# Attention followed by a two-layer MLP on one core: the first rows of k and q come in two pieces, k's first in float32 by another queue

## The chip, the cores and the metric

The kernel runs on one core of one Trainium2 chip. The metric is device time in microseconds (us) of one execution; less is better. Engines are named as in the profile: PE (TensorE, matmuls; PEld its weight loads), DVE (VectorE), ACT (ScalarE), POOL (GpSimd), SP (SyncE). PE writes to PSUM, in banks of 128 x 512 float32; DVE and ACT read PSUM; DMAs move data between device memory and SBUF.

## The reference

Sliding-window attention with a linear bias per head, then an MLP with an ELU between its two products. B = 8 batches, H = 8 heads, S = 576 positions, D = 64; 4608 tokens, 512 model columns, 2048 hidden columns. Inputs and output are float32.

```python
def _attn_ref(q, k, v):
    window, scale = 128, 1.0 / np.sqrt(D)
    scores = scale * np.matmul(q, k.transpose(0, 1, 3, 2))
    rel = pos[:, None] - pos[None, :]
    slopes = 2.0 ** (-8.0 * (np.arange(H) + 1) / H)
    bias = slopes[:, None, None] * (-np.abs(rel))[None, :, :]
    mask = (rel >= 0) & (rel < window)
    scores = np.where(mask, scores + bias[None], -1e9)
    attn = softmax(scores)                     # written out with max, exp and sum
    return np.matmul(attn, v)

x = attn_out.transpose(0, 2, 1, 3).reshape(B * S, H * D)
h = x @ w_in
g = np.where(h > 0, h, np.exp(np.minimum(h, 0)) - 1)
out = g @ w_out
```

## The kernel before, in words

**Attention.** A query block of 128 positions sees its own key block and the one before. The kernel goes by key blocks, called units: unit u takes keys 128u to 128u+127 and the 256 queries from 128u on (unit 3 takes the last rows with it). For batches 0 and 1 q and k are loaded with their rows in the partitions (tiles `s0`), turned on PE by 64 x 64 or 128 x 128 transposes into PSUM (`turn_first`, L136) and copied to the tiles QT and KT, with the head dimension in the partitions (L140). For the other batches DVE turns them (`turn_qk`).

The bias of batch 0 is added on PE: a matmul of a scaled identity (`SI`) with a table `RB` of distances and mask (`early_bias`, L183; `bias`, L166). Scores are added on top (`early_scores`, L191; `first_scores`, L176), ACT takes the exponential with the factor 1/8 out of PSUM (`early_expo`, L197 and L200; `first_expo`), and PE multiplies with v (`values`, L253), where a column of ones in v gives the sums, by which DVE divides (L259, L260). `turn` transposes the result (L289) and copies it to the tile `xT` (L290), block by block of 128 tokens. Later batches don't add the bias: they multiply the exponentials by a table `TAB` (`first_weigh`, `weigh`), which ACT makes from `RB` with one exponential per head (L471).

**MLP.** A step of `hidden` (L305) multiplies a block of `xT` with a part of w_in into one PSUM bank; in the early steps ACT takes the exponential (L315), POOL clamps it (L316) and DVE makes the ELU (`elu`, L323). `output` (L329), for the first 256 tokens, and after them `product` (L393, a form of the second product with seven half-size products in place of eight) multiply with w_out; `put` and `store` write the results by SP's queue.

**Order.** Nothing is scheduled by a planner: the order is written out by hand and each engine runs its instructions in that order. First comes a prologue: loads, masks, 22 matmuls on a constant tile that give PE something to do (`warm`), then units 0 and the first half of unit 1 of batch 0 in 128-query halves, with their values. Then a loop over numbered slots: each slot runs its `hidden` step, the ELU of the step before, the tasks that `at(slot, ...)` has put there, and the outputs. Steps 0 to 7 use w_in's four column parts for token blocks 0 and 1 in turn: steps 0 and 1 the first part, 2 and 3 the second, and so on.

**Loads at the start.** All go through POOL's queue, which casts float32 to float16 on the way, in this order: k rows 0 to 255, (iota for the masks), q rows 0 to 255, v blocks 0 and 1, w_in part 0, q rows 256 to 383, k rows 256 to 575, q rows 384 to 575, w_in parts 1 and 2, v block 2, and after some memsets w_in part 3 and v blocks 3 and 4. `split(b, w, part)` gives the pieces: start partition, number of partitions, rows to a partition, first row, and place in the tile. SP's queue does nothing before 41 us.

In the prologue k's two halves of heads (`half`) are turned into PSUM banks hp[0] and op and copied by DVE; q's into hp[1], copied by ACT, and av, copied by DVE. PSUM banks are named sp[0] to sp[3] (AB is the first two), hp[0], hp[1], av and op.

Of the kernel before, what the change touches and what calls it, by code (L numbers as in the profile page):

```python
# [18 lines left out]
def kernel(  # L19
# [9 lines left out]
    nc = tc.nc  # L29
# [60 lines left out]
    def split(b, w, part):  # L90

        if b == 0 and w == 1:
            return ((0, 64, 4, 0, 0), (64, 64, 5, 256, 0))[part]
        if b == 0:
            return ((0, 64, 4, 0, 0), (64, 64, 2, 256, 0), (64, 64, 3, 384, 2))[part]
        return ((0, 128, 4, 0, 0), (0, 64, 1, 512, 4))[part]

    def load_first(b, w, part):

        p0, n, m, r0, j0 = split(b, w, part)  # L100
        nc.gpsimd.dma_start(
            s0[b][p0:p0 + n, w, :, j0:j0 + m, :].rearrange("p h j d -> p h (j d)"),
            (q, k)[w][b, :, r0:r0 + n * m, :].rearrange("h (p j) d -> p h (j d)", j=m))

    def load_qk(b, w, g):
        if b not in st:
# [5 lines left out]
    def load_v(b, n):  # L112
        p = 128 if n < 4 else 64
        nc.gpsimd.dma_start(VP[b % 2][0:p, n, :, 0:D],  # L114
                            v[b, :, 128 * n:128 * n + p, :].rearrange("h p d -> p h d"))

    def load_wi(i):
        c = slice(512 * i, 512 * i + 512)
        nc.gpsimd.dma_start(w_in_sb[:, :, c], moe_w_in[:, c].rearrange("(c p) f -> p c f", p=128))
# [4 lines left out]
            moe_w_out[512 * i:512 * i + 512, :].rearrange("(c p) d -> p c d", p=128))  # L124


    def turn_first(b, w, part, half, bank, copy):

        p0, n, m, r0, j0 = split(b, w, part)
        nh = 4 if n * m < 256 else 2  # L130
        t = bank.bitcast(F16)[:, 0:nh * m * n].rearrange("p (x j r) -> p x j r", x=nh, j=m)
        r = slice(p0, p0 + n)
        for x in range(nh):
            for j in range(m):
                for hh in range(2):
                    nc.tensor.transpose(t[64 * hh:64 * hh + 64, x, j, :], s0[b][r, w, 4 * hh + nh * half + x, j0 + j, :],  # L136
                                        ident[r, r])
        t = t.rearrange("p x j r -> p x r j")
        o = (Q0, K0)[w][b][:, nh * half:nh * half + nh, r0:r0 + m * n]
        copy(o.rearrange("p x (r j) -> p x r j", j=m), t)  # L140
# [6 lines left out]
    nc.scalar.preload_act_table_set("natural_log_exp_and_others")  # L147

    with tc.manual_schedule():

# [26 lines left out]
        def early_bias(banks, c0):  # L179

            for x in range(4):
                for hh in range(2):
                    nc.tensor.matmul(banks[hh][:, 128 * x:128 * x + 128], SI[:, 4 * hh + x, :], RB[:, c0:c0 + 128],  # L183
                                     start=x == 0, stop=False, skip_group_check=True)

        def early_scores(banks, u, c0):
            k0, q0 = 128 * u, 128 * u + c0
            for x in range(4):
                for hh in range(2):
                    r = slice(64 * hh, 64 * hh + 64)  # L190
                    nc.tensor.matmul(banks[hh][:, 128 * x:128 * x + 128], kt_[0][r, x * S + k0:x * S + k0 + 128],  # L191
                                     Q0[0][r, x, q0:q0 + 128], start=False, stop=True, skip_group_check=True)

        def early_expo(banks, u, c0):
            e = ex_[u][:, 0:2048].rearrange("p (h c) -> p h c", h=8)[:, :, c0:c0 + 128]
            if banks is AB:
                nc.scalar.activation(e, spa.rearrange("p g (h c) -> p (g h) c", h=4), AF.Exp, scale=0.125)  # L197
                return
            for hh in range(2):
                nc.scalar.activation(e[:, 4 * hh:4 * hh + 4, :], banks[hh].rearrange("p (h c) -> p h c", h=4),  # L200
                                     AF.Exp, scale=0.125)
# [41 lines left out]
        def values(b, i, part, bank=av):  # L243

            m = 128 if i < 4 else 64
            banks = (part, part + 2) if b < 2 else (2 * part, 2 * part + 1)
            parts = [(3, 128, 3), (3, 192, 4)] if i == 4 else [(i, 0, i)] + ([(i - 1, 128, i - 1)] if i else [])
            a = bank[:, 0:4 * (D + 1)].rearrange("p (x h d) -> p x h d", x=2, h=2)
            for x, g in enumerate(banks):
                for h2 in range(2):  # L250
                    for j, (u, c, n) in enumerate(parts):
                        c += 512 * g + 256 * h2
                        nc.tensor.matmul(a[:, x, h2, :], ex_[u][:, c:c + 128], VP[b % 2][:, n, 2 * g + h2, 0:D + 1],  # L253
                                         start=j == 0, stop=j == len(parts) - 1)
            if part == 0:
                xnt[b, i] = work.tile([128, 4, 2, D], F16, name="xn", tag="xn", bufs=4)
            o = xnt[b, i][0:m, part::2, :, :] if b < 2 else xnt[b, i][0:m, 2 * part:2 * part + 2, :, :]
            r = work.tile([128, 2, 2], F32, name="rden", tag="rden", bufs=2)
            V.reciprocal(out=r[0:m], in_=a[0:m, :, :, D])  # L259
            V.tensor_tensor(out=o, in0=a[0:m, :, :, 0:D], in1=r[0:m].unsqueeze(3).broadcast_to([m, 2, 2, D]),  # L260
                            op=ALU.mult)
# [138 lines left out]
        def combine(n, what):  # L400
            late = n >= 2 * NTB - 2
            if what == "C11":
                add(tile_out(n, 0)[:, 0:256], kept(n, 1), place(n, 2))
                if late:
                    put(n, 0, 0, 256)
            elif what == "C12":
                add(tile_out(n, 0)[:, 256:512], kept(n, 6), place(n, 3))
                put(n, 0, 256 if late else 0, DO)
            else:
                add(tile_out(n, 1)[:, 256:512], kept(n, 7), kept(n, 5))  # L410
                if n == 2 * NTB - 2:
                    put(n, 1, 0, 256)
                put(n, 1, 256 if late else 0, DO)

        def put(n, i, c0, c1, queue=nc.sync):
            r = 256 * n + 128 * i
            queue.dma_start(out[r:r + 128, c0:c1], tile_out(n, i)[:, c0:c1])
# [11 lines left out]
        def warm(n, bank=op):  # L429
            for _ in range(n):  # L430
                nc.tensor.matmul(bank[:, 0:256], wz[:, 0:128], wz, start=True, stop=True)
# [3 lines left out]
        rel = fore[3][:, 1536:2048].bitcast(I32)  # L435
        far = fore[1][:, 0:256]
        V.memset(wz, 1.0)
        load_first(0, 1, 0)
        nc.gpsimd.iota(rel, pattern=[[1, 256]], base=0, channel_multiplier=-1)
        load_first(0, 0, 0)  # L440
        load_v(0, 0)
        load_v(0, 1)
        load_wi(0)
        load_first(0, 0, 1)
        load_first(0, 1, 1)
        load_first(0, 0, 2)
        load_wi(1)
        load_wi(2)
        load_v(0, 2)
# [17 lines left out]
            V.tensor_scalar(out=SI[:, h, :], in0=ident, scalar1=8.0 * slope[h], scalar2=None, op0=ALU.mult)  # L467
        V.memset(VP[0][:, :, :, D:D + 1], 1.0)

        for h in range(H):  # L470
            nc.scalar.activation(TAB[:, 0, h // 2, h % 2, :], RB[:, 0:256], AF.Exp, scale=slope[h])  # L471
        warm(22)
        turn_first(0, 1, 0, 0, hp[0], V.tensor_copy)
        turn_first(0, 1, 0, 1, op, V.tensor_copy)
        early_bias(AB, 0)
        turn_first(0, 0, 0, 0, hp[1], nc.scalar.copy)
        turn_first(0, 0, 0, 1, av, V.tensor_copy)
        V.tensor_copy(RB[:, 256:448], RB[:, 0:192])
        V.tensor_copy(RB[:, 448:512], RB[:, 0:64])
        V.tensor_copy(TAB[:, 1, :, :, 0:192], TAB[:, 0, :, :, 0:192])  # L480
        V.tensor_copy(TAB[:, 1, :, :, 192:256], TAB[:, 0, :, :, 0:64])
        early_bias(sp[2:4], 128)
        early_scores(AB, 0, 0)
        early_expo(AB, 0, 0)
        early_scores(sp[2:4], 0, 128)
        early_expo(sp[2:4], 0, 128)
        early_bias((hp[1], av), 0)
        early_scores((hp[1], av), 1, 0)
        early_expo((hp[1], av), 1, 0)
        values(0, 0, 0, hp[0])  # L490
# [2 lines left out]
        turn(0, 0, V.tensor_copy, hp[0])  # L493
        values(0, 1, 0)
        values(0, 1, 1, op)


        early, tasks, late, HID, OUT = {}, {}, {}, {}, {}

        def at(s, f, *a):  # L500
            tasks.setdefault(s, []).append((f, a))
# [39 lines left out]


        at(0, turn, 0, 1, V.tensor_copy)
        at(0, turn_first, 0, 0, 1, 0, sp[3], nc.scalar.copy)
        before(1, done, 0)
        at(1, early_bias, AB, 128)
        at(1, early_scores, AB, 1, 128)
        at(1, early_expo, AB, 1, 128)
        at(1, turn_first, 0, 1, 1, 0, av, V.tensor_copy)
        at(1, turn_first, 0, 1, 1, 1, sp[2], nc.scalar.copy)  # L550
        at(1, turn_first, 0, 0, 2, 0, hp[0], V.tensor_copy)
        for half in range(2):
            at(1, bias, 2, half, 3 * half)
        for half in range(2):
# [10 lines left out]
        at(5, first_scores, 0, 3, 1, 0)  # L565
        at(5, first_expo, 0, 3, 1, 0, 0, 256)
        at(5, done, 4)
        at(9, values, 0, 3, 0)
        at(9, values, 0, 3, 1, sp[3])
        at(10, values, 0, 4, 0)  # L570
# [135 lines left out]
```

## Time and profile before

| | us |
|---|---|
| median of 3 runs (lowest, highest) | 310.12 (309.92, 310.66) |
| the profiled execution | 310.72 |
| its span, from first to last instruction | 308.9 |
| PE busy in it | 300.8 |
| DVE, ACT, POOL busy | 258.0, 241.5, 108.5 |
| PE's first transpose of k, first of q | 6.00, 8.29 |
| MLP steps 0, 1, 2 start on PE | 13.61, 15.78, 20.37 |

A timeline line of the profile gives start, time busy, engine, source line and operation, the tile written and the tiles read, shape, count of merged instructions, and in brackets the idle time ahead of it with what ended it. DMA lines give the KB that are written and the time from issue to landing. Loads from POOL's queue are counted by their float16 size.

### The profile page before, as it was taken

What the parts mean: (1) busy time and instruction counts of PE and PEld (TensorE: products, weight loads), DVE (VectorE), ACT (ScalarE), POOL (GpSimd) and SP (SyncE); (2) the same over time, 40 slices, a digit from 0 to 9 for tenths busy, and PEclk for the clock granted to TensorE, in tenths of its full rate; (3) what the DMA queues carried; (4) which work ended last, traced back from release to release, by engine and by line L of the source; (5) the groups of instructions that cost most, each with busy time, mean ns of one, the idle gap of its engine ahead of it and who ended that gap; (6) DMA issues with size and microseconds to landing.
All of it is one profiled execution on the core that took longest, in us unless ns stands there. A gap on an engine that the chain in (4) does not pass through costs nothing.

```text
span 308.9 us, 9842 instructions
## 1 busy us (share of the span) xinstructions
PE 300.8 (97%) x4079; PEld 256.5 (83%) x4079; DVE 258.0 (84%) x499; ACT 241.5 (78%) x445; POOL 108.5 (35%) x163
## 2 busy tenths in 40 slices
PE   7899999999999999999999999999999999999996
PEld 5688775798788888988888888888899888888885
DVE  5646887988989999997989998989998788886783
ACT  4576678778889698879797889788988797968881
POOL 8938868274261415140707060806000101010000
PEclk9999999999999999999999999999999999999999
DMA  9999999999197929495979997999620302030103
GB/s 95 188 198 201 201 176 189 92 118 122 23 153 73 152 55 149 55 142 70 109 93 118 130 98 82 125 135 107 68 92 15 96 17 87 19 97 1 70 17 121
DMA packets 96941, 32.04 MB, mean 104 GB/s; under 512 B 83968, under 2 KB 92800, under 8 KB 96896
## 3 DMA queue, kind: packets, MB, share of 16 engines
q0 software_dynamic: 75920, 18.36, 64.8%
q1 hardware_dynamic: 20832, 12.98, 17.4%
q8 instruction: 32, 0.52, 0.7%
q14 instruction: 13, 0.11, 0.1%
q10 hardware_dynamic: 144, 0.07, 0.1%
HBM read 36.70 MB, written 9.44 MB: 149 GB/s over the span
## 4 chain that ended last, share of the span: by engine, by line
PE 76%; DVE 7%; ACT 6%; DMA 5%; issue 3%; POOL 2%; POOLq 0%; DVEq 0%; ACTq 0%
PE hp L305 34%; PE op L393 13%; PE av L393 12%; PE spa L225 4%; PE spa L271 3%; DVE g L323 2%; DMA s<-in_q_dram 2%; DMA VP<-in_v_dram 2%; ACT EX L236 2%; PE op L329 1%; DMA xT<-xn 1%; PE sp L393 1%; POOL e L316 1%; PE sp L305 1%; ACT e L315 1%
## 5 line engine op out<-in xcount | busy, mean ns | idle before, releaser
L305 PE MATMUL hp<-xT,wi 128*128 128x256 f16 (+3 forms) x1488 | 144.2, 245 | 1.2 <-DVE g L323 0.5
L305 PEld LDWEIGHTS <-wi 128*128 128x128 f16 x1600 | 119.7, 98 | 18.2 <-issue 6.1
L323 DVE SCALAR_TENSOR_TENSOR g<-e,hp 128x512 f16<-128x512 f32 x138 | 93.7, 679 | 22.2 <-ACT e L313 12.7
L316 POOL TENSOR_SCALAR e<-e 128x512 f32<-128x512 f32 x44 | 28.0, 635 | 158.9 <-ACT e L315 153.4
L312 ACT ACTIVATE e<-hp 128x512 f32<-128x512 f32 x98 | 58.6, 598 | 28.8 <-PE hp L305 24.3
L313 ACT ACTIVATE e<-e 128x512 f32<-128x512 f32 x100 | 63.1, 631 | 3.2
L393 PEld LDWEIGHTS <-S 128*128 128x128 f16 x544 | 51.2, 98 | 6.8 <-issue 0.6
L393 PEld LDWEIGHTS <-g 128*128 128x128 f16 x400 | 37.4, 98 | 4.6 <-issue 0.6
L241 DVE TENSOR_TENSOR EX<-EX,TAB 128x1024 f16<-128x1024 f16 x48 | 32.9, 686 | 6.1 <-ACT EX L236 4.0
L114 POOL DMA_DIRECT2D VP<-in_v_dram x40 | 34.3, 870 | 0.8 <-PE hp L305 0.3
L315 ACT ACTIVATE e<-hp 128x512 f32<-128x512 f32 x40 | 24.1, 601 | 10.6 <-PE hp L305 10.6
L393 PE MATMUL op<-T,S 128*128 128x256 f16 x200 | 30.0, 273 | 0.1
L233 ACT ACTIVATE EX<-spa 128x1024 f16<-128x1024 f32 x24 | 24.6, 1025 | 3.7 <-PE spa L225 3.4
L393 PE MATMUL av<-T,S 128*128 128x256 f16 x176 | 26.4, 272 | 0.1
L236 ACT ACTIVATE EX<-sp 128x512 f16<-128x512 f32 x48 | 26.0, 596 | 0.0
L354 DVE TENSOR_TENSOR S<-g 128x1024 f16<-128x1024 f16 (+2 forms) x35 | 23.5, 672 | 0.8 <-PE op L393 0.2
L393 PE MATMUL op<-wo,g 128*128 128x256 f16 x128 | 19.2, 272 | 0.1
L393 PE MATMUL av<-wo,g 128*128 128x256 f16 x120 | 18.0, 272 | 0.0
L277 DVE TENSOR_TENSOR xn<-spa,rden 128x512 f16<-128x512 f32 x24 | 16.6, 691 | 0.8
L108 POOL DMA_DIRECT2D st<-in_k_dram x24 | 16.2, 686 | 2.8 <-DMA s<-in_q_dram 1.7
L108 POOL DMA_DIRECT2D st<-in_q_dram x24 | 15.9, 666 | 0.8 <-DMA VP<-in_v_dram 0.7
L271 PE MATMUL spa<-VP,EX 128*128 128x65 f16 x336 | 15.3, 193 | 0.1
(139 smaller groups left out, 382.5 us busy)
## 6 DMA issues: line engine op xcount, KB each, us to landing
out_dram<-ob SPq DMA_DIRECT2D x32, 256.0 KB, 2.8
VP<-in_v_dram POOLq DMA_DIRECT2D x32, 128.0 KB, 5.7
st<-in_k_dram POOLq DMA_DIRECT2D x24, 144.0 KB, 5.2
st<-in_q_dram POOLq DMA_DIRECT2D x24, 144.0 KB, 6.3
wi<-in_moe_w_in_dram POOLq DMA_DIRECT2D x4, 512.0 KB, 11.1
wo<-in_moe_w_out_dram POOLq DMA_DIRECT2D x4, 512.0 KB, 9.7
out_dram<-ob SPq DMA_DIRECT2D x7, 128.0 KB, 1.7
VP<-in_v_dram POOLq DMA_DIRECT2D x8, 64.0 KB, 5.9
```

Of the source, the lines that this page charges most:

```text
L108: nc.gpsimd.dma_start(st[b][32 * g:32 * g + 32, w, :, :, :, :].rearrange("p h n j d -> p (h n) (j d)"), (q, k)[w][b, 2 * g:2 * g + 2, :, : ...
L114: nc.gpsimd.dma_start(VP[b % 2][0:p, n, :, 0:D], v[b, :, 128 * n:128 * n + p, :].rearrange("h p d -> p h d"))
L233: nc.scalar.activation(unit(b, u)[:, 0:2, :, :], spa.rearrange("p g (h c) -> p g h c", h=2), AF.Exp, scale=0.125)
L236: nc.scalar.activation(unit(b, u)[:, g, :, :], sp[g].rearrange("p (h c) -> p h c", h=2), AF.Exp, scale=0.125)
L241: V.tensor_tensor(out=e, in0=e, in1=TAB[:, int(u == 3), 2 * gp:2 * gp + 2, :, :], op=ALU.mult)
L305: nc.tensor.matmul(p[:, l * w + u0:l * w + u1], w_in_sb[:, c, fc * 128:(fc + 1) * 128], xT[:, c, x0:x0 + u1 - u0], start=(c == 0), stop=(c ...
L312: nc.scalar.activation(e[:, 0:n], p[:, 0:n], AF.Relu, scale=-1.0)
L313: nc.scalar.activation(e[:, 0:n], e[:, 0:n], AF.Exp, scale=-1.0)
L315: nc.scalar.activation(e[:, 0:n], p[:, 0:n], AF.Exp)
L316: nc.gpsimd.tensor_scalar(out=e[:, 0:n], in0=e[:, 0:n], scalar1=1.0, scalar2=0.0, op0=ALU.min, op1=ALU.max)
L323: V.scalar_tensor_tensor(out=gs[t][:, f0:f0 + nf, c0:c0 + w], in0=sh(es.pop((t, c0, f0))), scalar=1.0, in1=sh(hps.pop((t, c0, f0))), op0=A ...
L393: nc.tensor.matmul(o, a[:, j, :], b[:, j, :], start=j == 0 and i in (1, 2, 5), stop=j == 7, skip_group_check=True)
```

## The change

- Batch 0's first 256 rows of k and q come in two pieces of 128 rows each (64 partitions, two rows to a partition). The first piece of k goes by SP's queue, without a cast, into a tile `raw` of the pool that later holds q and k of batch 2 and on (`load_raw`); DVE and ACT each cast half of its heads to float16 (`cook`). The other three pieces go by POOL's queue.
- POOL makes the iota before its first load. After it come q's first piece, k's second, q's second, then v and w_in as before.
- 14 warm matmuls stand in place of 22, and two more stand between the pieces. Three of the eight tables of `TAB` are made ahead of the casts and five after the first values.
- The first unit is scored by halves of its queries: the first half as soon as the first pieces are turned, the second half and unit 1's first half after the second pieces.
- The bias of unit 1's second half moves from slot 1 to the end of the prologue, ahead of step 0. The two copies that make the second form of `TAB` move from the prologue to slot 3, on DVE.
- Near the end, one store of 256 columns and its neighbour become one store of 512 (`combine`, n = 16).

```diff
     def split(b, w, part):
         if b == 0 and w == 1:
-            return ((0, 64, 4, 0, 0), (64, 64, 5, 256, 0))[part]
+            return ((0, 64, 2, 0, 0), (0, 64, 2, 128, 2), (64, 64, 5, 256, 0))[part]
         if b == 0:
-            return ((0, 64, 4, 0, 0), (64, 64, 2, 256, 0), (64, 64, 3, 384, 2))[part]
+            return ((0, 64, 2, 0, 0), (0, 64, 2, 128, 2), (64, 64, 2, 256, 0), (64, 64, 3, 384, 2))[part]
...
+    raw = stage.tile([128, 2, 2, R, 2, D], F16, name="st")
+    raw = raw.rearrange("p a b n j d -> p (a b n j d)").bitcast(F32)[0:64, 0:1024].rearrange("p (h j d) -> p h j d", h=H, j=2)
+
+    def load_raw():
+        nc.sync.dma_start(raw.rearrange("p h j d -> p h (j d)"), k[0, :, 0:128, :].rearrange("h (p j) d -> p h (j d)", j=2))
+
+    def cook(half, copy):
+        copy(*[t.rearrange("p (a b x) j d -> p b a x (j d)", a=2, b=2)[:, half] for t in (s0[0][0:64, 1, :, 0:2, :], raw)])
...
-    def turn_first(b, w, part, half, bank, copy):
+    def turn_first(b, w, part, half, bank, copy, nh=None):
...
-        nh = 4 if n * m < 256 else 2
+        nh = nh or (4 if n * m < 256 else 2)
...
     with tc.manual_schedule():
+        load_raw()
...
-                if n == 2 * NTB - 2:
-                    put(n, 1, 0, 256)
-                put(n, 1, 256 if late else 0, DO)
+                put(n, 1, 256 if n == 2 * NTB - 1 else 0, DO)
...
         V.memset(wz, 1.0)
-        load_first(0, 1, 0)
         nc.gpsimd.iota(rel, pattern=[[1, 256]], base=0, channel_multiplier=-1)
         load_first(0, 0, 0)
+        load_first(0, 1, 1)
+        load_first(0, 0, 1)
         load_v(0, 0)
         load_v(0, 1)
         load_wi(0)
-        load_first(0, 0, 1)
-        load_first(0, 1, 1)
         load_first(0, 0, 2)
+        load_first(0, 1, 2)
+        load_first(0, 0, 3)
...
-        for h in range(H):
-            nc.scalar.activation(TAB[:, 0, h // 2, h % 2, :], RB[:, 0:256], AF.Exp, scale=slope[h])
-        warm(22)
-        turn_first(0, 1, 0, 0, hp[0], V.tensor_copy)
-        turn_first(0, 1, 0, 1, op, V.tensor_copy)
+        def table(h0, h1):
+            for h in range(h0, h1):
+                nc.scalar.activation(TAB[:, 0, h // 2, h % 2, :], RB[:, 0:256], AF.Exp, scale=slope[h])
+
+        table(0, 3)
+        warm(14, sp[3])
+        cook(0, V.tensor_copy)
+        cook(1, nc.scalar.copy)
+        turn_first(0, 1, 0, 0, hp[0], V.tensor_copy, 2)
+        turn_first(0, 1, 0, 1, op, nc.scalar.copy, 2)
         early_bias(AB, 0)
-        turn_first(0, 0, 0, 0, hp[1], nc.scalar.copy)
-        turn_first(0, 0, 0, 1, av, V.tensor_copy)
-        V.tensor_copy(RB[:, 256:448], RB[:, 0:192])
-        V.tensor_copy(RB[:, 448:512], RB[:, 0:64])
-        V.tensor_copy(TAB[:, 1, :, :, 0:192], TAB[:, 0, :, :, 0:192])
-        V.tensor_copy(TAB[:, 1, :, :, 192:256], TAB[:, 0, :, :, 0:64])
+        turn_first(0, 0, 0, 0, hp[1], V.tensor_copy, 2)
+        turn_first(0, 0, 0, 1, av, nc.scalar.copy, 2)
         early_bias(sp[2:4], 128)
         early_scores(AB, 0, 0)
         early_expo(AB, 0, 0)
+        turn_first(0, 1, 1, 0, op, V.tensor_copy)
+        early_bias((hp[1], av), 0)
+        warm(2, hp[0])
+        turn_first(0, 0, 1, 0, hp[0], V.tensor_copy, 2)
+        turn_first(0, 0, 1, 1, op, nc.scalar.copy, 2)
+        V.tensor_copy(RB[:, 256:448], RB[:, 0:192])
+        V.tensor_copy(RB[:, 448:512], RB[:, 0:64])
         early_scores(sp[2:4], 0, 128)
         early_expo(sp[2:4], 0, 128)
-        early_bias((hp[1], av), 0)
         early_scores((hp[1], av), 1, 0)
         early_expo((hp[1], av), 1, 0)
...
         values(0, 1, 1, op)
+        early_bias(AB, 128)
+        table(3, H)
...
-        at(0, turn_first, 0, 0, 1, 0, sp[3], nc.scalar.copy)
+        at(0, turn_first, 0, 0, 2, 0, sp[3], nc.scalar.copy)
...
-        at(1, early_bias, AB, 128)
...
+        at(3, V.tensor_copy, TAB[:, 1, :, :, 0:192], TAB[:, 0, :, :, 0:192])
+        at(3, V.tensor_copy, TAB[:, 1, :, :, 192:256], TAB[:, 0, :, :, 0:64])
```

More of the change, by code (lines that the diff above doesn't have):

```diff
@@ L543 @@
         at(0, turn, 0, 1, V.tensor_copy)
-        at(0, turn_first, 0, 0, 1, 0, sp[3], nc.scalar.copy)
+        at(0, turn_first, 0, 0, 2, 0, sp[3], nc.scalar.copy)
         before(1, done, 0)
-        at(1, early_bias, AB, 128)
         at(1, early_scores, AB, 1, 128)
         at(1, early_expo, AB, 1, 128)
-        at(1, turn_first, 0, 1, 1, 0, av, V.tensor_copy)
-        at(1, turn_first, 0, 1, 1, 1, sp[2], nc.scalar.copy)
-        at(1, turn_first, 0, 0, 2, 0, hp[0], V.tensor_copy)
+        at(1, turn_first, 0, 1, 2, 0, av, V.tensor_copy)
+        at(1, turn_first, 0, 1, 2, 1, sp[2], nc.scalar.copy)
+        at(1, turn_first, 0, 0, 3, 0, hp[0], V.tensor_copy)
         for half in range(2):
```

## The prediction, made before the kernel was run

> **What bounds the kernel now.** I read the page first, then the waits of the first 14 us, the chain of waits up to 45 us, the timeline up to 26 us, and the DMA answers for small stretches. Engines, share of the span (page, part 1), and DMA load in 40 slices (part 2):
>
> ```profile
> PE 300.8 (97%) x4079; PEld 256.5 (83%) x4079; DVE 258.0 (84%) x499; ACT 241.5 (78%) x445; POOL 108.5 (35%) x163
> ...
> DMA  9999999999197929495979997999620302030103
> ```
>
> TensorE (PE) is full nearly everywhere, so the end moves only if PE's whole stream starts sooner and nothing later holds it to the clock on the wall. The DMA engines are full for ten slices (77 us), so landings could hold it. Timeline of the start (start, us busy, engine, line, what; in brackets the idle time before):
>
> ```profile
> 1.19 4.88 PE L431 MATMUL op<-T 128*128 128x256 f16 x22 [1.19 <-DVE T L437]
> ...
> 2.18 0.37 POOL L439 IOTA T<- 128x256 int32 x1
> ...
> 3.90 2.56 ACT L471 ACTIVATE TAB<-T 128x256 f16<-128x256 f16 x8 [1.87 <-DVE T L464]
> ...
> 6.62 0.62 PE L183 MATMUL spa<-T 128*128 128x128 f16 x8
> ...
> 8.29 0.44 PE L136 MATMUL hp<-ident,s 64*64 64x64 f16 x16 [1.04 <-DMA s<-in_q_dram]
> ...
> 10.09 1.02 ACT L197 ACTIVATE EX<-spa 128x1024 f16<-128x1024 f32 x1 [0.74 <-PE spa L191]
> ...
> 12.44 0.63 ACT L200 ACTIVATE EX<-av 128x512 f16<-128x512 f32 x1
> ...
> 13.61 1.05 PE L305 MATMUL hp<-xT,wi 128*128 128x128 f16 x16
> ...
> 15.78 1.05 PE L305 MATMUL hp<-xT,wi 128*128 128x128 f16 x16
> ```
>
> (Groups overlap: 16 transposes last 0.44, but the next group starts after 0.27; the other 0.17 is the way out of PE.) PE waits for q until 8.29; then scores, five exponentials on ACT to 13.07, values, and MLP steps 0 and 1 at 13.61 and 15.78. The chain of waits agrees on what holds the start:
>
> ```profile
> 2.47 5.78 DMA s<-in_q_dram
> ```
>
> Steps 2, 4 and 6 start at 20.37, 23.03 and 26.67. Issue plus landing put the weights at 12.6 (wi 0), 18.2 (wi 1), 21.4 (wi 2) and 24.4 (wi 3): 1.0, 2.1, 1.6 and 2.2 us ahead of their users. That slack is the ceiling of any gain here.
>
> **Method.** I lined up the instructions of the first 30 us of both kernels, engine by engine in program order, with durations from the rows. For the kernel before this gives 13.29 for the last exponential's end (trace 13.07), 13.82, 15.86 and 20.16 for steps 0, 1, 2 (13.61, 15.78, 20.37), so I subtract reckoning from reckoning.
>
> **Masks.** The iota goes ahead of POOL's DMAs. POOL's first of these started at 1.25 after 0.80 idle, so the iota ends between 1.2 and 1.6; I take 1.5. In the trace the bias row (RB) is ready 1.32 after it and the eight diagonals 2.46 after: 2.8 and 4.0. Three tables (2.56/8 = 0.32 each) end at 3.8 on ACT.
>
> **Raw k by SyncE.** No row shows a plain load by this queue. Its stores of 256 KB land 2.3 us after issue when the engines are quiet (85.6) and 5.2 to 6.2 when full. SP's first wait ends at 0.7 and the engines are idle until 2.5, so I take 3.0, with 2.4 and 6.9 as ends. The casts (512 values a lane; rows of that size take 0.42 to 0.69 on DVE, 0.59 on ACT) run from 3.8 to 3.9, by ACT and DVE at once: done 4.5. A landing up to 3.8 is hidden by tables and diagonals; one at 5.0 takes 0.6 of the gain, one at 6.0 all of it. Behind the waiting casts stand only the copies of these pieces (on ACT also the first exponential), so nothing off the path is held; SP has nothing else to do before 41 us.
>
> **PE to 6.0.** The warm matmuls start 0.222 apart (4.88/22): 14 end at 4.3. PE then idles 0.25. The granted clock (part 2, and the windows) reads full from the first us, but the rows show a slow clock at first: 256 columns took 420 ns each in the warm group and 273 ns later (L393), and the bias at 6.62, 8 x 128 columns in 0.62 - 0.17, is paced at 56 ns, half the 111 that the warm group paid for 128. If it switches at 6.0 again, k's 16 transposes cost 0.54 instead of 0.27 and the first bias 0.9 instead of 0.45: 4.55 to 6.0.
>
> **q's first piece** is issued after the iota, at 1.5. The k load of before landed 4.2 after issue; half the bytes at its 188 GB/s save 0.7, a busier start may add as much: 5.0 to 5.9, hidden by PE's work to 6.0.
>
> **From 6.0.** Transposes 0.27 and 0.17 until the result is out; copies of 256 columns 0.4 (half of 0.69, with its fixed part): 6.9. Scores 0.3, out at 7.4; the first exponential ends at 8.47 (11.29 reckoned before). Meanwhile PE turns k's second piece (to 7.5), adds a bias (0.45) and two warm matmuls (0.22), and at 8.2 turns q's second piece; its second half waits until DVE has emptied bank op (8.41), and ACT's copy ends at 9.2. The other scores follow, and four exponentials of 0.5 end at 11.86, against 13.29: 1.43 gained. Issued at 2.2 and 2.9, the second pieces must land by 8.2; at 4.2 to 5.8 after issue that is 6.4 to 8.7.
>
> **To step 0 and beyond.** The bias moved ahead of step 0 takes 0.44 there: step 0 gains 0.99. Five tables (1.6) move behind the exponentials; ACT has until 13.9, and ends them at 13.5: nothing. At step 1 the gain is 1.23, at step 2 1.54, since the bias is gone from between. At step 3 the two table copies of 0.79 and 0.69 come back on DVE, which is idle 0.88 there (the wait ahead of L259 at 24.38), and the chain of waits runs through DVE from there to 29.8. They fill about 1.4: 0.5 too much. **Left: 1.54 - 0.47 = 1.07 us.** In step 0's place (13.82 - 0.99 = 12.83) wi 0 at 12.6 just clears, as wi 2 does at step 4 (21.5 against 21.4).
>
> **Landings.** POOL's queue has 128 KB less ahead of wi 0 (-0.7 at 188 GB/s), one more piece to issue (0.7, of which the iota's earlier place gives back 0.3; wi 0 waits in the queue anyway), and 512-byte packets become 256. Row: 188 GB/s with 512-byte packets (5 to 6 us), 174 with 256-byte ones (48.5 to 50): 8%, on 384 KB 0.2. v's blocks 0 and 1, issued at 3.14 and 4.04, landed at 8.6 and 9.4; with the same +0.3 block 0 is there before the first values (9.85 here, 11.17 before). So -0.5 to +0.3; at +0.3 the gain falls to about 0.8. [...]
>
> Later stages give the shift through: batch 1's q, issued at 32.17 and landing 9.3 later, is used at 46.15, 4.7 us of slack. The store merged near the end saves a DMA issue of 0.33 on SP, which is not what ends there: nothing.
>
> **Sum.** The profiled execution took 310.72 (span 308.9 and 1.8 around it), 0.6 above the median of 310.12. 310.72 - 1.07 = 309.65; the same shift on the median gives 309.05, rounded to 309.0.
>
> **Rivals.** *Late clock (slower).* Before, 4.88 us of unbroken matmuls stood ahead of the first fast group; now 3.1, then waits. If PE stays slow past 6.0, every bias (0.45), transpose group (0.27) and score group (0.24) to the first values doubles, on the path. From 6.0 to q's second piece PE has 0.27 + 0.45 + 0.30 + 0.27 + 0.45 + 0.22 + 0.27 = 2.23; doubled, about 0.85 of the addition goes into waits for copies and 1.4 into the end. So a switch at 8.5 eats the gain, one at 9.4 makes it 0.3 slower, and one at 12.8, with the scores, values and turn of block 0 slow too (some 2.0, 1.2 of it into waits), 1.15 slower: 311.3. For it: the slow rows last until the whole 4.88 are over. Against: PE's slow work itself fills the gaps. [...]
>
> *Late pieces (little change).* Before's q took 5.78 where k took 4.2. If the second pieces land at 9.0 the gain is 0.5, with wi 0 at +0.3 likewise: 309.6.
>
> *More gain.* If the clock switches by 5.0, PE is through its first bias at 5.1 and 0.45 more is won; landings 0.5 sooner let step 4 follow: 1.5 to 2, 308.3.
>
> *The change does less than it says*: raw k is of no use if it lands after 6.0; that ends in the second rival at best.
>
> **How the numbers follow.** Forecast 0.42 (308.5 to 309.6), late clock 0.25, more gain 0.17, late pieces 0.16. A measurement here can tell 0.3%, 0.93 us: below 309.19 is faster, above 311.05 slower. Faster: 0.33 of the forecast, 0.17, 0.05 of late pieces. Slower: 0.20, the late clock from a switch past about 11.8. Same: the rest, 0.25. The range of 307.9 to 311.3 leaves out about one in ten on either side. The likeliest case's own range is 308.5 to 309.6.
>
> **What would show it.** Right: casts done by 4.6; warm matmuls ending at 4.3; first exponential of unit 0 starting near 7.5, step 0 near 12.7, step 2 near 18.8, step 8 about 1.1 ahead of 28.46. The late clock shows as bias groups of 128 columns at 0.11 us apiece after 6.0. Late pieces show as PE waiting on s or the raw tile. I am wrong if step 0 is ahead and the end is not (the shift is given back after 30 us), or if the waits on wi grow by what step 0 gains.

## The result, and the profile after

The change made the kernel slower: median 312.92 us (309.71 to 313.46, 20 runs) against 310.01 (309.48 to 310.75, 20 runs) for the kernel before; the ratio of the runs is 1.0077, with an interval of 1.0058 to 1.0096. The median is 2.9 us up where the prediction had 1.1 down. The runs lie on levels: 14 between 312.6 and 313.5, four at 311.1 to 311.4, two at 309.7 and 310.0. The mean granted clock that each run reports is 0.999 or 1.000 for all but three: the runs at 311.38, 311.38 and 311.44 have 0.989.

The profiled execution took 312.92, with a span of 311.1 (before 308.9). Its page, part 1, shows the same engines with nearly the same shares; PE has 2.3 us more busy time with six instructions fewer, so PE works slower somewhere:

```profile
span 311.1 us, 9839 instructions
...
PE 303.1 (97%) x4073; PEld 258.6 (83%) x4073; DVE 258.7 (83%) x501; ACT 242.6 (78%) x448; POOL 109.0 (35%) x164
```

The timeline of the start after the change, with the lines that answer to those of before (L442 is the warm group, L147 the transposes, L196 the bias, L318 the MLP steps):

```profile
1.19 3.17 PE L442 MATMUL sp<-T 128*128 128x256 f16 x14 [1.19 <-DVE T L448]
...
4.67 0.90 DVE L114 CAST s<-st 64x512 f16<-64x512 f32 x1 [1.00 <-DMA st<-in_k_dram]
...
5.63 0.42 PE L147 MATMUL hp<-ident,s 64*64 64x64 f16 x8 [1.27 <-DVE s L114]
...
6.20 1.04 PE L196 MATMUL spa<-T 128*128 128x128 f16 x8
...
9.35 1.02 ACT L210 ACTIVATE EX<-spa 128x1024 f16<-128x1024 f32 x1 [1.14 <-PE spa L204]
...
14.21 0.62 ACT L213 ACTIVATE EX<-av 128x512 f16<-128x512 f32 x1
...
15.98 0.72 PE L196 MATMUL spa<-T 128*128 128x128 f16 x8
...
16.54 1.06 PE L318 MATMUL hp<-xT,wi 128*128 128x128 f16 x16
...
18.33 1.05 PE L318 MATMUL hp<-xT,wi 128*128 128x128 f16 x16
```

The bias group is the clock's ruler: the same eight matmuls of 128 columns took 0.62 at 6.62 before and take 1.04 at 6.20 now. The group at 7.73 is slow as well (1.04), and so is the one at 9.80 (its matmuls start 0.11 apart, in the kernel before 0.06), the one at 15.98 is in between (0.72), and from step 0 on, at 16.54, PE runs as before (1.06 a step against 1.05). So the slow clock lasted to about 16.2 instead of 6.0. The trace's own record of the granted clock agrees: its first entry, full clock, stands at 16.21, and in the profile before at 5.96. Ahead of the first entry there is none, and the clock column of the profile's views then reads 1.00 although PE is slow. The first exponential does start 0.7 us earlier than before (9.35 against 10.09), but the last one ends at 14.83 instead of 13.07 and step 0 starts 2.9 later. Step 2, at 22.50 (before 20.37), is 2.1 later, and the span ends 2.2 later: what was lost at the start is kept to the end.

### The profile page after: what moved, and what is told of

Its sections match the earlier page's. It is cut to its first block, busy times and chain, and to the rows that moved or that the text cites. A ratio compares the mean times of both kernels' runs of the same rounds, so it can differ in the third digit from the quotient of the medians.

```text
span 311.1 us, 9839 instructions
## 1 busy us (share of the span) xinstructions
PE 303.1 (97%) x4073; PEld 258.6 (83%) x4073; DVE 258.7 (83%) x501; ACT 242.6 (78%) x448; POOL 109.0 (35%) x164
## 3 DMA queue, kind: packets, MB, share of 16 engines
q1 hardware_dynamic: 21216, 13.24, 17.2%
## 4 chain that ended last, share of the span: by engine, by line
PE 73%; DMA 7%; DVE 6%; ACT 5%; POOL 4%; issue 3%; POOLq 0%; DVEq 0%
PE hp L318 33%; PE op L406 13%; PE av L406 12%; DMA VP<-in_v_dram 6%; PE spa L238 3%; PE spa L284 3%; DVE g L336 2%; ACT e L328 2%; POOL e L329 2%; POOL VP L125 2%; PE sp L406 1%; ACT EX L249 1%; DMA st<-in_k_dram 1%; PE sp L266 1%; DVE S L367 1%
## 5 line engine op out<-in xcount | busy, mean ns | idle before, releaser
L318 PE MATMUL hp<-xT,wi 128*128 128x256 f16 (+3 forms) x1488 | 144.3, 245 | 1.0 <-DVE g L336 0.5
L318 PEld LDWEIGHTS <-wi 128*128 128x128 f16 x1600 | 119.6, 98 | 18.3 <-issue 6.6
```

The costliest lines, as they stand in the source:

```text
L318: nc.tensor.matmul(p[:, l * w + u0:l * w + u1], w_in_sb[:, c, fc * 128:(fc + 1) * 128], xT[:, c, x0:x0 + u1 - u0], start=(c == 0), stop=(c ...
```

## The experiments

The theory: 14 warm matmuls (3.2 us) with a pause behind them no longer bring the fast clock at 6 us; it then comes later, at a time that differs between executions, and that makes the levels. By my estimate the later times lie in steps of about 3.4 us: between the first entries of the two profiles there are 10.25 us, three times 3.42. (Two profiles below, whose clock changes three times, fit that, each within itself: the changes are at 4.40, 14.64 and 21.46 with 17 warm matmuls, and at 6.83, 17.07 and 20.49 with w_in late. The gaps are 10.24 and 6.82, and 10.24 and 3.42, which are 3, 2, 3 and 1 times 3.41.) The rival: the pieces and loads themselves (raw k, casts, small packets) are late. Ratios are to the kernel before, run on the same chip.

**The warm matmuls alone, both ways.** In the changed kernel:

```diff
-        warm(14, sp[3])
+        warm(22, sp[3])
```

> The changed kernel with 22 warm matmuls again in place of 14, nothing else. Clock theory: PE is busy without a break to 6.1 us, the fast clock comes at about 6.0 in every run, as before the change; step 0 starts when w_in part 0 lands (13.7 us) instead of 16.5, step 2 near 19.7, and the time falls from 312.9 to 310.0 (309.5 to 310.5), with the three levels of the changed kernel's runs (313.1, 311.3, 309.8) gone. Rival, late pieces: k's first piece lands at 4.65 and the cast ends at 5.6 whatever PE does, and eight more matmuls push the transposes to 6.1; the time stays at 312.5 to 313.5.

Measured: eleven runs at 309.8 to 310.9, median 310.06, ratio 0.9996 (0.9980 to 1.0012). The twelfth took 767.8; it was the profiled one, and neither it nor its profile is read here. The theory holds: eight matmuls that compute nothing give back the 2.9 us, as far as the interval can tell. That the clock is what they bring is seen in the next kernel with 22 (the one with the table copies in slot 2, below), where the ruler is fast at 6.00 and the clock's first entry stands at 4.34:

```profile
1.19 4.10 PE L442 MATMUL sp<-T 128*128 128x256 f16 x22 [1.19 <-DVE T L448]
...
6.00 0.62 PE L196 MATMUL spa<-T 128*128 128x128 f16 x8
```

And in the kernel before, the other way:

```diff
-        warm(22)
+        warm(14)
```

> The kernel before with 14 warm matmuls in place of 22, nothing else; the 8 matmuls write nothing that is used. Clock theory: PE idles from 4.3 to k's landing at 5.5, the 3.4 us stretch that ends at 6.0 is no longer full, and the fast clock comes at 9.4, 12.8 or 16.2 us: 310.6, 311.5 or 312.9 by my reckoning, and a wider spread between runs than the kernel before has. Rival, the clock is not what the change lost: PE has spare time before 8.3 us and the time stays at 310.0, or falls.

Measured: median 312.00, ratio 1.0056 (1.0032 to 1.0079), runs spread from 310.6 to 313.8. So the slowdown comes without any of the other edits. Its timeline shows the slow ruler again (1.04 at 6.50), the clock's first entry stands at 12.02, at none of the three times that I had reckoned, and step 0 starts at 14.89 instead of 13.61:

```profile
1.20 3.17 PE L431 MATMUL op<-T 128*128 128x256 f16 x14 [1.20 <-DVE T L437]
5.50 0.63 PE L136 MATMUL hp<-ident,s 64*64 64x64 f16 x16 [1.14 <-DMA s<-in_k_dram]
...
6.50 1.04 PE L183 MATMUL spa<-T 128*128 128x128 f16 x8
...
14.89 1.05 PE L305 MATMUL hp<-xT,wi 128*128 128x128 f16 x16
```

**Doses between.** 20 and 17 warm matmuls in the changed kernel, nothing else.

> The changed kernel with 20 warm matmuls in place of 14: they end at 5.6 us, when the casts end, so PE has no break and nothing is put off. [...] Rival, the number 22 has another worth than the unbroken work: the time stays above 311.5.

> The changed kernel with 17 warm matmuls in place of 14; they end at 5.0 us and PE has 0.7 us of break. Clock theory: between the two. [...] Rival, only the sum of PE work by 9 us counts: no slower than with 20.

Measured: 20 gives 310.29, ratio 0.9993 (0.9971 to 1.0016), nine of twelve runs at 309.6 to 310.4. 17 gives 311.76, ratio 1.0026 (0.9992 to 1.0060): six runs at 309.6 to 311.0 and six at 312.5 to 314.0. The median with 17 alone isn't told apart from the kernel before; the two groups of runs are. I had put the medians at 310.0 to 310.6 and 311.3 to 312.7, and a quarter of the runs with 17 near 310; half of them were. So the dose acts as the theory has it, somewhat sooner than I put it.

The first entry of the clock's record in all profiles that can be read:

| warm matmuls | full clock from (us), profile by profile, some with the other edits below |
|---|---|
| 14 | 16.21 (changed kernel), 12.02 (kernel before) |
| 17 | 4.40 |
| 20 | 4.71, 5.34, 5.75, 6.83, 6.88 |
| 22 | 4.34, 5.67 (changed kernel), 4.47, 5.70, 5.96 (kernel before) |

So from 17 on the fast clock came between 4.3 and 6.9 us, at a place that differs between executions of one kernel (4.71 and 5.34, with 20 and the copies in slot 2), and with 14, in both profiles, not before 12. Why 14 was enough in two runs of twenty is not shown: neither run has a profile.

The timeline with 20 shows the forecast path at work: no pause of PE ahead of the transposes, the ruler fast at 6.04, step 0 at 13.28, and step 8 at 27.44, 1.02 ahead of the profile before (28.46). That execution took 309.74.

```profile
1.19 4.45 PE L442 MATMUL sp<-T 128*128 128x256 f16 x20 [1.19 <-DVE T L448]
...
6.04 0.62 PE L196 MATMUL spa<-T 128*128 128x128 f16 x8
...
13.28 1.06 PE L318 MATMUL hp<-xT,wi 128*128 128x128 f16 x16
```

The profiled execution with 17 (313.96) shows something else. Its clock was fast early (from 4.40, so 17 sufficed here too), and then fell back. Windows of PE (stretch, its length, busy, instructions, granted clock, DMA share, GB/s), and the step behind it:

```profile
11.20:14.64 3.44, 1.75 (x29) 1.00 1.39 180
14.64:18.00 3.36, 2.93 (x38) 0.50 1.32 204
18.00:21.50 3.50, 3.50 (x72) 0.51 1.48 195
21.50:25.00 3.50, 3.42 (x69) 1.00 1.63 189
```

```profile
15.07 1.89 PE L318 MATMUL hp<-xT,wi 128*128 128x128 f16 x16 [1.68 <-DMA wi<-in_moe_w_in_dram]
```

PE waited 1.68 us for w_in part 0, was busy for only half of the 3.44 us to 14.64, and ran at half clock for the next seven: step 0's matmuls took 1.89 instead of 1.05.

**The table copies.** With 22 warm matmuls, and then with 20, slot 2 instead of slot 3:

```diff
-        at(3, V.tensor_copy, TAB[:, 1, :, :, 0:192], TAB[:, 0, :, :, 0:192])
-        at(3, V.tensor_copy, TAB[:, 1, :, :, 192:256], TAB[:, 0, :, :, 0:64])
+        at(2, V.tensor_copy, TAB[:, 1, :, :, 0:192], TAB[:, 0, :, :, 0:192])
+        at(2, V.tensor_copy, TAB[:, 1, :, :, 192:256], TAB[:, 0, :, :, 0:64])
```

> As the changed kernel with 22 warm matmuls, and the two copies for the second form of TAB in slot 2 instead of slot 3. Theory: in slot 3 they hold up the values of block 2 by 0.5 us on DVE; in slot 2 DVE is idle for over 2 us. 0.3 to 0.5 us faster than the same kernel with them in slot 3, 309.5 to 309.8 if that one takes 310.0. Rival: another wait (w_in part 2, landing at 22.1) takes over, and the two are equal within 0.1.

> 20 warm matmuls and the two table copies in slot 2 instead of slot 3: the candidate that may beat both. Against 20 warm matmuls alone it tells what the copies in slot 3 cost: 0.3 to 0.5 by the trace of DVE. Theory: 309.6 to 310.0 in the median, 0 to 0.4 below the kernel before. Rival: equal to 20 warm matmuls alone, because PE waits for w_in (landing at 13.7 and 19.7) anyway.

Measured: with 22, 310.35, ratio 1.0008 (0.9989 to 1.0027), not told apart from 0.9996; with 20, 310.10, ratio 0.9984 (0.9967 to 1.0000), against 0.9993. The traces say it better: from step 2 to step 8 the kernel with 20 takes 19.24 to 27.44, 8.20 us, and with the copies in slot 2 19.19 to 27.28, 8.09, as before the change (20.37 to 28.46). In this pair of profiles the copies in slot 3 cost 0.11, not the 0.47 of the prediction.

**Which load is late.** In the changed kernel's profile w_in part 0, issued at 5.29, lands 8.5 later, at 13.8; before, at 12.6. k's first piece by POOL with 22 warm matmuls:

```diff
-        load_raw()
...
+        load_first(0, 1, 0)
         load_first(0, 0, 0)
         load_first(0, 1, 1)
...
-        cook(0, V.tensor_copy)
-        cook(1, nc.scalar.copy)
```

> As the changed kernel with 22 warm matmuls, and k's first piece by POOL's queue with its cast, right after the iota, in place of SyncE's float32 load and the two casts on ACT and DVE. In the changed kernel w_in part 0 lands at 13.7 us, 1.1 later than before. Theory A, the four small pieces in 256-byte packets cost the time: it lands at 13.7 or later here too (one more piece in POOL's queue, up to 0.7) and the time is 0 to 0.7 above the kernel with 22. Theory B, SyncE's packets get in the way: it lands near 12.7 again and the time is 0.3 to 0.6 below the kernel with 22. k's own transposes start at 6.1 in both, since the piece lands by 5.5.

Measured: 311.37, ratio 1.0053 (1.0028 to 1.0078), 1.3 above the kernel with 22, more than either theory had. w_in part 0 lands 8.3 after 5.96, at 14.3, and PE waits 0.67 for it. Four of the twelve runs (312.95 to 313.7) have a mean granted clock of 0.995, the others 0.999 or more, so part of the cost is a clock that fell back, as with 17. By its time SyncE's load, which takes one piece out of POOL's queue, is worth having; nothing shows its packets to be in the way.

Packets of 512 bytes in place of 256, on top of the kernel with 20 and the copies in slot 2 (`split`, first and second pieces):

```diff
         if b == 0 and w == 1:
-            return ((0, 64, 2, 0, 0), (0, 64, 2, 128, 2), (64, 64, 5, 256, 0))[part]
+            return ((0, 64, 2, 0, 0), (0, 32, 4, 128, 2), (64, 64, 5, 256, 0))[part]
         if b == 0:
-            return ((0, 64, 2, 0, 0), (0, 64, 2, 128, 2), (64, 64, 2, 256, 0), (64, 64, 3, 384, 2))[part]
+            return ((0, 32, 4, 0, 0), (32, 32, 4, 128, 0), (64, 64, 2, 256, 0), (64, 64, 3, 384, 2))[part]
```

> 20 warm matmuls, the table copies in slot 2, and POOL's three small pieces with four rows to a partition on 32 partitions in place of two rows on 64: packets of 512 bytes, half as many, and 16 transposes more for each piece (0.27 us each). Theory, packets of 256 bytes are why w_in part 0 lands 1.1 us later than before the change: it lands at 13.0 or sooner, w_in part 1 at 18.5, and the extra transposes cost up to 0.5; the time is 0.5 below to 0.2 above that of the kernel with the same warm matmuls and copies. Rival, the order and number of the loads and not the packets: w_in part 0 stays at 13.5 to 14.3 and the time is 0.2 to 0.6 above.

Measured: 314.61, ratio 1.0131 (1.0097 to 1.0164). In its profile w_in part 0 still lands at 14.1 (5.27 + 8.8), so larger packets did not bring it sooner; one landing, among landings that differ by 2 us and more, does not exclude them. The kernel is 4.5 above the one that it is built on. About 1.5 stands already at step 0 (14.78 against 13.24): the extra transposes, and a clock that came at 6.88 instead of 4.71. The rest, with a pause of PE of 1.15 between steps 1 and 2 in it, is left open.

w_in part 0 behind the next pieces of q and k, with 20 warm matmuls and the copies in slot 2, to see whether its landing is the floor:

```diff
-        load_wi(0)
         load_first(0, 0, 2)
         load_first(0, 1, 2)
+        load_wi(0)
         load_first(0, 0, 3)
```

> As that kernel, with w_in part 0 issued after the third piece of q and the rest of k (448 KB more ahead of it in POOL's queue: 2.3 us at 190 GB/s). Theory, the landing of w_in part 0 is the floor of step 0 and of the gain: it lands near 15 us, PE waits 1.5 to 2 us for it, and the time is 1.2 to 2 us higher (311.2 to 312); in some runs PE's clock falls back to half in that wait, and those take 313 to 314.5. Rival, the time is set elsewhere: it stays within 0.4 of the kernel with the usual order.

Measured: 313.31 (311.51 to 314.61), ratio 1.0091 (1.0056 to 1.0126). It lands at 15.6 (6.63 + 9.0); the timeline shows the wait and then half clock at step 1, as in the run with 17:

```profile
15.71 1.07 PE L318 MATMUL hp<-xT,wi 128*128 128x128 f16 x16 [1.83 <-DMA wi<-in_moe_w_in_dram]
...
17.51 1.87 PE L318 MATMUL hp<-xT,wi 128*128 128x128 f16 x16
```

The floor is there, and missing it costs more than the wait, because the clock goes too: 2.9 to 3.2 us above the two measurements of the kernel that it is built on, for a landing 1.3 to 3.3 later. The runs' own clock says the same: the one run with a mean granted clock of 1.000 took 311.51, three with 0.995 took 313.1 to 313.3, two with 0.988 took 314.3 and 314.6.

**Controls and what is left.** The kernel before, unchanged:

> The kernel before, unchanged: a control, and a second profile of it. The forecast was built on one profiled execution (310.72) that was 0.6 above the median. Theory: that execution's wait for q (to 8.24 us) was a long draw; here q lands at 7.0 to 8.0 us, step 0 starts before 13.4, and the profiled time is 309.4 to 310.2. Rival: q lands at 8.2 again and step 0 starts at 13.6. The ratio to the same kernel is 1 within 0.002.

Measured: 310.51, ratio 0.9996 (0.9974 to 1.0019); runs from 309.5 to 311.8. q lands at 8.0 and step 0 starts at 13.40: between theory and rival, nearer to the rival. Its profiled execution took 310.70.

The kernel before with the pause ahead of q filled:

```diff
         early_bias(AB, 0)
+        warm(6, av)
         turn_first(0, 0, 0, 0, hp[1], nc.scalar.copy)
```

> The kernel before with six more warm matmuls between the first bias and q's transposes, where PE waits for q from 7.0 to 8.3 us; they take 0.7 to 1.3 us there. Theory, the slow runs of the kernel before (up to 312.5) come from the clock too: the spread shrinks, no run is above 311, the median is 0.1 to 0.4 lower than before. Rival: PE's pace before 8.3 us doesn't matter in the kernel before, and the median is the same within 0.15 with the same tail.

Measured: 310.32, ratio 0.9988 (0.9966 to 1.0010), runs from 309.7 to 311.0. No run is above 311; the median isn't told apart. What the tail of the kernel before is, its runs' clock shows: of the 29 on this chip, seven of the eight above 311.5 have a mean granted clock of 0.989 to 0.994, and all the others 0.999 or more. So by my estimate the clock fell back later in the execution in those seven: a slow start alone reads 1.000, as the profiled run of the changed kernel does. That the six matmuls prevent this is not shown firmly: with such a fall in 9 of the 41 runs of the kernel before on this chip, twelve runs without one come by chance about once in twenty. In its profile q landed at 6.9 (2.47 + 4.4), not 8.2, and the transposes of q started at 7.71, when the warm matmuls were done: q's landing varies by over 1 us, so part of the wait for q in the profile before was that execution's own.

The changed kernel with 20 warm matmuls and the copies in slot 2, again:

> The changed kernel with 20 warm matmuls and the table copies in slot 2, a second time on another chip, since its interval (0.9967 to 1.0000 of the kernel before) touched 1. Theory: median 309.8 to 310.2, 0.998 to 1.000 of the kernel before; step 0 starts when w_in part 0 has landed, between 12.3 and 14 us, and the time follows it.

Measured: 310.42, ratio 0.9998 (0.9979 to 1.0017). The median is above the 309.8 to 310.2 that I expected, the ratio within. Its profiled execution shows why the early scores aren't worth more even with the fast clock. PE is through with the values and the moved bias by 13.4 and waits for the weights:

```profile
14.38 1.07 PE L318 MATMUL hp<-xT,wi 128*128 128x128 f16 x16 [0.99 <-DMA wi<-in_moe_w_in_dram]
```

Landings of w_in part 0 in the profiles, issue plus time to landing, with the change's order of loads: 13.8, 13.7, 12.6, 15.0, 12.3, 14.3; with the order of before: 12.6, 12.3, 12.9, 11.5. The mean is 13.6 against 12.3, with a wide spread. Neither larger packets (14.1) nor leaving out SyncE's load (14.3) brought it sooner, in one profile each; what in the order delays it stays open. No version here is shown to beat the kernel before: the two best ratios, 0.9984 and 0.9988, have intervals that reach 1.

## Why the prediction was wrong

**The step that failed** is "If it switches at 6.0 again" in the part on PE to 6.0. The sum of 1.07 stood on it, and it had no row behind it: the profile before showed a switch after 4.88 us of unbroken matmuls and nothing about 3.2. The rival that came true was there, with its place and its sign, at 0.25. The doses lean the way of the rival: with 14 warm matmuls (3.17 us) two of 20 runs took what a clock at 6 us gives, with 17 (3.8 us at the slow pace of 0.222) six did by their times and the profiled one by its trace, seven of twelve, with 20 (4.45) nine of twelve were fast, with 22 (4.88) all eleven. No length shows as a threshold: the clock rose at 4.34 and 4.40, 3.15 and 3.21 us after the first matmul, and in other executions, with 20, only at 6.83 and 6.88. What is measured is that more unbroken work made an early switch likelier here.

Against that rival I had set "PE's slow work itself fills the gaps". By busy time it did fill them, and the clock stayed slow: after the change PE was busy 3.41 of 3.41 us from 5.98 to 9.39, and 3.10 of the next 3.41. What differs from the kernel before is the stretch ahead of these, 2.15 of 3.42 us, which there was full:

```profile
2.54:5.96 3.42, 3.42 (x17) 1.00 1.07 133
```

After the change:

```profile
2.56:5.98 3.42, 2.15 (x23) 1.00 1.32 165
5.98:9.39 3.41, 3.41 (x58) 1.00 1.75 143
9.39:12.80 3.41, 3.10 (x56) 1.00 1.32 180
12.80:16.21 3.41, 3.41 (x44) 1.00 1.39 195
```

These busy shares count modelled ends. The stretch to 9.39 was full and the clock stayed slow; the one to 16.21 was full and the clock rose at its end. What made the difference no run here shows.

**The size of the rival** was cut short. I priced a switch up to 12.8 us, 1.15 us slower, and let the range end at 311.3. The profiled switch came at 16.21, 3.4 us later than the last that I priced; step 0 was 2.93 later than before and the median 2.9.

The level in the middle does not fit so simply. My price for a switch at 12.8, 311.3, is its time, but three of its four runs have a mean granted clock of 0.989, where the profiled execution with its slow start reports 1.000 and the fall-back of 6.8 us with 17 gave 0.988. So these three had about 7 us at half clock later in the execution (my estimate, from that pair). What their start was like, and whether any run switched at 9.4 or 12.8, no profile shows.

**The other terms.** Raw k landed 3.9 us after its issue at 0.74, at 4.65, not 3.0, and its first packets moved only at about 2.2. The store that I took as a row for quiet engines (2.3 us at 85.6) was issued while they were busy, at a DMA share of 1.56 from 85.5 to 86.0, and so was no such row. The casts took 0.90 on DVE and 0.62 on ACT, not 0.6, so the transposes started at 5.6 instead of 4.55. q's first piece (5.0 to 5.9 forecast) landed at 5.4, the second pieces (6.4 to 8.7) at 6.6 and 7.5: right. The iota ended at 1.2, at the early end. The table copies were put too high, 0.47 for 0.11. w_in part 0 was forecast at -0.5 to +0.3 and came at +1.2 in that profile.

**Where the forecast gain is.** With 20 warm matmuls, one profiled execution took 309.74 and had steps 2 and 8 ahead of the first profile by 1.13 and 1.02; the forecast was 1.54 and 1.07, and 309.65 for the profiled execution. That the end agrees is partly luck: the gain at step 2 was 0.4 short, and the table copies cost 0.36 less than forecast. And it needs w_in part 0 by about 13.2; in other executions it came at 13.7 to 15.0, and the median gains nothing that can be told. I saw that w_in had 1.0 us of slack, called it the ceiling, and then took one execution's landing, give or take half a microsecond, as fixed.

## What to carry to other kernels

Warm-up matmuls are not filler to be trimmed to what the next load needs: here 14 in place of 22 cost 2.9 us in the changed kernel and made the kernel before 1.0056 times as long. Cut them only with the time measured, and look at the pace of a known group, not at a busy share, to see where the clock switched. When runs of one kernel lie on levels, look for something that switches, read each run's own clock, and price the latest switch, not only the first (16.21 here, where my prices ended at 12.8). A wait that a change removes is worth at most the slack of the next thing that must land, and both should be read from more than one execution.

## What the runs showed of the hardware that I had not expected

- The clock fell back inside the kernel in two profiles in which PE waited 1.68 and 1.83 us for one load, w_in part 0. After 3.41 us with PE busy for 1.72 (17 warm matmuls, 11.23 to 14.64) 6.8 us at half clock (0.50 and 0.51 in the windows) followed, and after 1.58 (w_in late, 13.66 to 17.07) 3.4 us (0.51). With 2.37 busy of 3.41 (12.17 to 15.58, second measurement of the kernel with 20 and the copies in slot 2, with a wait of 0.99) the full clock stayed.
- The granted clock column read 1.00 through the slow start (to 5.96 before, to 16.21 after the change, and from 4 to 12 in the kernel before with 14) and 0.50 in the later fall-back: these records have no entry before the first switch, so at the start only the matmuls' pace and the time of the first entry tell.
- A 256 KB load by SyncE's queue, issued at 0.7 with the DMA engines idle (no packet moving from 0.7 to 0.8), took 3.9 to 4.1 us to land in the profiles, where stores of that size in the kernel before landed 2.3 us after issue at the quickest.
- The time at which the same load lands differs by 2 us between two executions of the same program (w_in part 0 at 12.3 and 14.3, with 20 warm matmuls and the copies in slot 2).
